# Attention, mixer and feed-forward in one kernel: 51 shifted due times in a planned order of work

## Chip, cores and metric

The kernel runs on one core of one Trainium2 chip. The metric is the device time of one execution in microseconds (us); less is better. The time before is a median of three runs.

## The reference

Three parts follow one another, all in float32. B = 8 batches, 8 heads, S = 576 positions, width 512.

```python
# attention: phi(x) = [exp(p), exp(-p)], p = x @ w_phi - max|x @ w_phi|
kv = einsum('bhsf,bhsd->bhfd', phi(k), v);  z = sum_s phi(k)
out = einsum('bhsf,bhfd->bhsd', phi(q), kv) / (einsum('bhsf,bhf->bhs', phi(q), z) + 1e-6)
# mixer: causal convolution of 5 taps as a gate
x = (sigmoid(conv(x, conv_w)) * (x @ w_val)) @ w_out
# Fourier mixing, layer norm, feed-forward of width 2048
u = x + real(fft(fft(x, axis=1), axis=2))
out = u + relu(layernorm(u) @ w_ch1) @ w_ch2
```

## The kernel before, in words

Products that need full precision are made of three reduced ones: a tile is split in a high half (a copy on ScalarE, `o_hi`) and a low half (a subtraction on VectorE or GpSimd, `o_lo`), and `mm3` issues high x high, high x low and low x high.

*The attention loop* (`run_attention`) is an order written out by hand: 49 stages, in each of which the projection, the exponentials, the products `kv` and `num`, the division and the transposes of different groups of the sequence overlap. Beside it the weights are converted.

*The joint list* is all that comes after: the last of the attention (`note_tail`: transposes `yt`, products `kv`, three times `num`, four times the transposes `xt` and their copy to `xT`), the mixer and the Fourier mixing for eight batches (`note_mix`), and the feed-forward part for five blocks of columns (`note_mlp`; its products are made with seven instead of eight quarter products, tiles `x`, `y`, `z`, `cx`, `cy`). The note functions don't issue anything. Each call of `op` appends a step to a list: which engines may do it (m TensorE, v VectorE, a ScalarE, p GpSimd, d a load or store), how long it is thought to take, the function that issues it, and the keys that it reads and writes. The list has some 4,600 steps. Steps are numbered in the order in which they are noted.

*The planner* (`place_ops`) turns the list into one order per engine. It works out from the keys which step needs which. A pass from the back then gives each step a due time, the latest at which it may start if all that follows it is to fit before the end; the pass is run twice, the second time with the ends of the five stages that the first one found. Then the list is dealt out from the front: each time, for every engine, of the steps that can start earliest the one with the earliest due time is a candidate, and the candidate with the earliest start of all is placed. A step that may run on VectorE or GpSimd goes to whichever takes it first. The order found is issued as it stands; each engine works its own instructions off in that order and waits where an input isn't there. So a due time sets which of several ready steps goes first, and nothing else.

The planner begins with `free`, the time at which each engine becomes free, and `key_at`, the time at which keys from before the list are ready. Both are zero here, although at that point the attention loop's last instructions still run.

In the mixer each batch's activations are split into the tile `xh` (four chunks, one buffer). For each of four column groups `val` = `xh` x `wv` is computed in two banks, multiplied by the gate `acc` (five taps on ScalarE and VectorE, then a sigmoid) into `gv`, folded into `gs` and split into `ge`. The products of `ge` with `wo`, then those with the Fourier tables, go to a ring of four banks `ps`. The layer norm of the first block (`ln_first`, in two halves) runs between the later batches; it reads back `u`, which was stored in `u_scr`.

`u<-x`, `f<-fs`, `ge<-gs`, `xh<-xf` and `r<-r` in the rows are such sums and splits. `ws<-s_scr` is a load of weights whose sums GpSimd makes.

Nearly all steps of the list have line 64 in the profile, as one helper issues them; they are told apart by their tiles.

Of the kernel before, what the change touches and what calls it, by code (L numbers as in the profile page):

```python
# [9 lines left out]
F32 = mybir.dt.float32  # L10
# [5 lines left out]
ACTF = mybir.ActivationFunctionType  # L16
# [51 lines left out]
def attention_moe_mixer_kernel(  # L68
# [19 lines left out]
    pe, act, vec, gps = (Issue(x) for x in (nc.tensor, nc.scalar, nc.vector, nc.gpsimd))  # L88
    mm = pe.matmul

    def pool(stack, name, bufs, space=None, side=None):
        kw = {} if space is None else {"space": space}
        if side is not None:
            kw["side"] = side
        if space is not DRAM:
            kw["reuse_waits"] = "tile"
        return stack.enter_context(tc.tile_pool(name=name, bufs=bufs, **kw))
# [96 lines left out]
    NG, CH = 3, 3  # L194
# [5 lines left out]
    early = ExitStack()  # L200
# [22 lines left out]
    sm_p = pool(att, "sm", 2)  # L223
# [14 lines left out]
    kvps = {}  # L238
    kvT = {}
    xs = {}  # L240
    xT = {}
# [39 lines left out]

    KV_PARTS = [[[(0, 0), (1, 1), (2, 2)]], [[(3, 0), (4, 1)], [(5, 1), (6, 2)]], [[(7, 0), (8, 1), (9, 2)]]]

    def emit_KV(i, part):
        u, g = divmod(i, NG)
        tv = vraw[u % 2]
        e = kE[i]
        for slot, j in KV_PARTS[g][part]:
            b = slot // 5
            if slot % 5 == 0:  # L290
                kvps[u, b] = ps_kv.tile([128, 4, 66], F32, tag="kv", name="kv")
            t = kvps[u, b]
            for h in range(2):
                for a in range(2):
                    w = 2 * h + a
                    for p in HALVES:
                        mm(t[p, w, :], e[:, a, h, j, p], tv[:, h, slot, :],
                           start=slot % 5 == 0 and w == 0, stop=slot % 5 == 4 and w == 3, skip_group_check=True)
            if slot % 5 == 4:
                if b == 0:  # L300
                    kvT[u] = sm_p.tile([128, 4, 2, 65], F32, tag="kvT", name="kvT")
                act.activation(out=kvT[u][:, :, b, :], in_=kvps.pop((u, b))[:, :, 0:65], func=ACTF.Copy)
        if part == len(KV_PARTS[g]) - 1:
            kE.pop(i)

    def emit_yT(i):
        y = yq.pop((i, 1))
        t = ps_tr.tile([128, 2, 512], F32, tag="tr", name="yt")
        for h in range(2):
            for j in range(CH):  # L310
                nc.tensor.transpose(t[:, h, j * F:(j + 1) * F], y[:, h, j, :], ident)  # L311
        yq[i, 2] = t

    def emit_qE(i, a):
        if a == 0:
            qE[i] = qe_p.tile([128, 2, 2, CH, F], F32, tag="qe", name="qe")
        t = yq[i, 2] if a == 0 else yq.pop((i, 2))
        act.activation(out=qE[i][:, a], in_=chunks(t), func=ACTF.Exp, scale=(1.0, -1.0)[a])

    def emit_num(i):  # L320
        u, g = divmod(i, NG)
        e = qE.pop(i)
        kt = kvT[u]
        nm[i] = t = ps_nm.tile([128, 2 * CH, 66], F32, tag="nm", name="nm")
        for j in range(CH):
            c = CH * g + j
            for h in range(2):
                for a in range(2):
                    for b, p in enumerate(HALVES):
                        if c != 4:  # L330
                            b = 0 if c < 4 else 1
                        mm(t[p, 2 * j + h, 0:65], e[:, a, h, j, p], kt[:, 2 * h + a, b, :],
                           start=(a == 0), stop=(a == 1))

    def emit_X(i):
        t = nm.pop(i)
        xs[i] = x = xs_p.tile([128, CH, 2, D], F32, tag="xs", name="xs")
        r = sm_p.tile([128, 2 * CH, 1], F32, tag="r", name="r")
        nc.vector.tensor_scalar(out=r, in0=t[:, :, D:D + 1], scalar1=1e-6, scalar2=None, op0=ALU.add)
        nc.vector.reciprocal(out=r, in_=r)  # L340
        nc.vector.tensor_tensor(
            out=x.rearrange("p c h d -> p (c h) d"), in0=t[:, :, 0:D], in1=r.to_broadcast([128, 2 * CH, D]), op=ALU.mult,
        )
# [8 lines left out]
    def emit_xT(i, e):  # L352
        t = xs.pop((i, 1))
        xT[i] = xT_p.tile([128, CH * F], F32, tag="xT", name="xT")
        (hi_dve if e == "v" else hi_act)(xT[i], t[:, 0, 0:CH * F])
# [307 lines left out]
    def stage(k):  # L663
        n = k if isinstance(k, str) else k[0]
        if n == "ge":
            n += str(k[1])
        if k == ("ps", 4) or k[:2] == ("x2", 1):
            return 3, 3
        return STAGES.get(n, (0, 4))
# [8 lines left out]
    def op(e, cols, fn, reads, writes, dur=None, more=0.0, two=False, table=None, kb=0):  # L678


        two = two and not any(k in BANKS or k[0] in BANKS for k in reads)
        if dur is None:
            dur = {k: COST[k][0] + COST[k][1] * cols / 1000 for k in e}
        else:
            dur = {e: dur}
        at = [stage(k) for k in reads + writes]
        ops.append((dur, fn, reads, writes, more, two, max([a for a, b in at], default=0), min([b for a, b in at], default=4), table, here[0], kb))
# [471 lines left out]
                c2 = c2_units(t, pair)  # L1159
        drain(c2)  # L1160

    key_at = {}
    free = dict.fromkeys("mvapdxw", 0.0)

    def place_ops():
        n = len(ops)
# [21 lines left out]
        part = [o[6] for o in ops]  # L1188
# [4 lines left out]
        due = [0.0] * n  # L1193
# [3 lines left out]
        for i in reversed(range(n)):  # L1197
            now -= ops[i][0].get("m", 0)
            if "m" in ops[i][0] or ops[i][9]:
                place[i] = now  # L1200
        for _ in range(2):
            till = dict.fromkeys("mvapdw", total)
            rest = [len(s) for s in succ]
            heap = []

            def open_up(i):
                late = min([due[s] - lat for s in succ[i]] + [ends[last[i]], total]) - ops[i][4]
                if ops[i][10]:
                    late = min(late, till["w"] - K["bw"] * ops[i][10])
                late = min(late, place[i] + min(ops[i][0].values()))  # L1210
                heapq.heappush(heap, (-late, -i))

            for i in reversed(range(n)):
                if not rest[i]:
                    open_up(i)
            while heap:
                late, i = (-k for k in heapq.heappop(heap))
                e = max(ops[i][0], key=lambda e: min(late, till[e]) - ops[i][0][e])
                due[i] = till[e] = min(late, till[e]) - ops[i][0][e]
                if ops[i][10]:  # L1220
                    till["w"] = min(till["w"], late + K["bw"] * ops[i][10]) - K["bw"] * ops[i][10]
                for p in pred[i]:
                    rest[p] -= 1
                    if not rest[p]:
                        open_up(p)
            ends = [min(due[i] for i in range(n) if part[i] > k) if k < 4 else 1e9 for k in range(5)]
        left = [len(p) for p in pred]
        ready = {e: set() for e in "mvapd"}
        at = [max([key_at.get(k, 0.0) + lat for k in ops[i][2] + ops[i][3]], default=0.0) for i in range(n)]
# [25 lines left out]
        for _ in range(n):  # L1255
            best = None
            for e, q in ready.items():
# [14 lines left out]
                i, t0 = min(((i, t) for i, t in cand if t <= t0 + K["win"]), key=lambda c: (due[c[0]], c[0]))  # L1272
# [41 lines left out]
    def note_tail():  # L1314
        nk = ["kvT"]

        def kv(i):
            op("m", 0, lambda e: emit_KV(i, 0), ["early"], ["kv"], 24 * 0.058)

        def yt(i):  # L1320
            op("m", 0, lambda e: emit_yT(i), ["early"], ["tr"], 2 * CH * 0.11)
            for a in range(2):
                op("a", 256 * CH, lambda e, a=a: emit_qE(i, a), ["tr", "att"], [("qe", i, a)], table=ACTF.Exp)

        def num(i):
            op("m", 0, lambda e: emit_num(i), nk * (i % NG > 0) + [("qe", i, 0), ("qe", i, 1), "att"], ["nm"], 8 * CH * 0.058)

        def x(i):
            op("v", 0, lambda e: emit_X(i), ["nm", "att"], [("xs", i % 3)], 0.19 + 0.2 + 0.07 + 0.13 * CH)

        def xt(i):
            op("m", 0, lambda e: emit_XT(i, ps_tr, "tr"), [("xs", i % 3), "att"], ["tr"], CH * 0.11)
            op("a", 128 * CH, lambda e: emit_xT(i, "a"), ["tr"], [("xT", i % 2)])
            t = Late(lambda: xT[i])
            o_dma([(o, t[:, k]) for b, o, k in x_parts(i)], [("xT", i % 2)], [("x_scr", b) for b, o, k in x_parts(i)], 192)

        yt(TOT - 1)
        kv(TOT - 1)
        num(TOT - 3)
        x(TOT - 3)  # L1340
        xt(TOT - 4)
        for i in range(TOT - 3, TOT):
            yield
            xt(i)
            if i + 1 < TOT:
                num(i + 1)
                x(i + 1)

    def run_attention():
# [8 lines left out]
        with tc.manual_schedule():  # L1358
            for st in range(TOT + 1):
# [6 lines left out]
                if two:  # L1366
                    emit_KV(st - 2, 0)
# [5 lines left out]
                if at(2):  # L1373
                    emit_KV(st - 2, int(two))
# [167 lines left out]
```

## Time and the profile before

| | before |
|---|---|
| median of three runs | 1323.23 us (1321.36 to 1324.6) |
| the profiled execution's own time | 1319.18 us |
| its span, first to last instruction | 1317.1 us |
| TensorE busy | 1285.5 us, 98% |
| VectorE busy | 1134.1 us, 86% |
| ScalarE busy | 919.0 us, 70% |
| GpSimd busy | 791.9 us, 60% |
| mean granted TensorE clock | 0.996 |

Engines in rows: PE is TensorE's matmuls, PEld its weight loads, DVE VectorE, ACT ScalarE, POOL GpSimd, SPq the queue that issues loads and stores. Times in the rows are from the span's start. The busy share of an engine that nobody waits for says nothing about the time; idle time of TensorE does.

### The profile page before, as it was taken

The numbers are of one execution on the slowest core, as the hardware profiler recorded it, in microseconds if no ns is written. First come the engines' busy times: TensorE is split into PE (matmuls) and PEld (weight loads), VectorE is DVE, ScalarE is ACT, GpSimd is POOL, SyncE is SP. The second block draws the span as 40 slices with busy tenths as digits, with TensorE's granted clock in tenths as the row PEclk, the third lists the DMA queues.
The fourth block names the chain that finished last, engine by engine and source line by source line (L and its number), as shares of the span: only waits on it lengthen the run. The fifth ranks groups of instructions, "written<-read, shape, count | busy, mean of one in ns | idle before, by whom it ended". The sixth has DMA issues, their size and how long they took to land.

```text
span 1317.1 us, 30740 instructions
## 1 busy us (share of the span) xinstructions
PE 1285.5 (98%) x11952; PEld 1183.3 (90%) x11952; DVE 1134.1 (86%) x1771; ACT 919.0 (70%) x1718; POOL 791.9 (60%) x661
## 2 busy tenths in 40 slices
PE   8999999998999998999999999999999999999998
PEld 7999899988999998998888888888888888889997
DVE  6888888878889889779989989998989888888785
ACT  6888999774556546466867687767677676777662
POOL 4868889333557666464665755597458856583321
PEclk9999999998999999999999999999999999999999
DMA  8689999522342442528433653356333743345322
GB/s 309 207 287 308 319 300 296 189 83 89 137 165 88 147 155 89 177 89 276 138 102 102 222 159 104 103 160 218 104 103 117 241 123 100 105 149 182 105 84 89
DMA packets 147005, 214.62 MB, mean 163 GB/s; under 512 B 18854, under 2 KB 105382, under 8 KB 146860
## 3 DMA queue, kind: packets, MB, share of 16 engines
q1 hardware_dynamic: 142400, 203.06, 47.5%
q10 hardware_dynamic: 4460, 9.62, 2.0%
q8 instruction: 93, 1.52, 0.5%
q14 instruction: 52, 0.43, 0.1%
HBM read 165.63 MB, written 46.99 MB: 161 GB/s over the span
## 4 chain that ended last, share of the span: by engine, by line
PE 86%; DVE 6%; ACT 4%; DMA 2%; issue 1%; POOL 0%; SPq 0%; DVEq 0%; POOLq 0%; ACTq 0%
PE x L64 15%; PE cx L64 15%; PE ps L64 12%; PE cy L64 11%; PE y L64 8%; PE val L64 5%; PE kv L64 5%; PE pj L64 5%; PE nm L64 4%; PE z L64 4%; DVE acc L64 2%; PE yt L311 2%; PE xt L349 1%; ACT qe L64 1%; DMA r<-s_scr 1%
## 5 line engine op out<-in xcount | busy, mean ns | idle before, releaser
L64 POOL TENSOR_TENSOR r<-r 128x256 fp32r<-128x256 f32 (+1 forms) x301 | 293.4, 992 | 245.6 <-ACT r L64 229.2
L64 ACT ACTIVATE r<-r 128x256 fp32r<-128x256 f32 (+1 forms) x420 | 195.3, 487 | 53.4 <-DMA r<-s_scr 49.7
L64 PE MATMUL x<-un,r 128*128 128x462 f32 (+1 forms) x960 | 221.2, 371 | 2.2 <-ACT c L64 1.4
L64 PE MATMUL cx<-h,r 128*128 128x462 f32 (+1 forms) x960 | 213.9, 371 | 1.1 <-DVE acc L64 1.1
L64 PEld LDWEIGHTS x<-un,r 128*128 128x128 f32 x960 | 180.4, 188 | 23.5 <-ACT c L64 1.8
L64 PEld LDWEIGHTS cx<-h,r 128*128 128x128 f32 x960 | 180.2, 188 | 22.1 <-DVE acc L64 1.8
L64 PE MATMUL cy<-h,r 128*128 128x462 f32 (+1 forms) x720 | 159.9, 370 | 0.0
L64 PEld LDWEIGHTS cy<-h,r 128*128 128x128 f32 x720 | 135.3, 188 | 15.1
L64 PE MATMUL val<-xh,wv 128*128 128x290 f32 x768 | 118.0, 303 | 10.6 <-DVE gs L64 4.7
L64 PEld LDWEIGHTS val<-xh,wv 128*128 128x128 f32 x768 | 108.5, 193 | 13.7 <-DVE gs L64 5.6
L64 PE MATMUL y<-un,r 128*128 128x462 f32 (+1 forms) x480 | 113.9, 372 | 0.4 <-DVE h L64 0.4
L64 PE MATMUL ps<-ge,wo 128*128 128x290 f32 x768 | 107.3, 297 | 2.0 <-DVE x L64 1.1
L64 PEld LDWEIGHTS ps<-ge,wo 128*128 128x128 f32 x768 | 104.5, 189 | 2.8 <-DVE x L64 1.3
L270 DVE TENSOR_REDUCE m<-pj 128x6 f32<-128x768 f32 x96 | 91.5, 953 | 15.4 <-PE pj L64 14.8
L64 PEld LDWEIGHTS y<-un,r 128*128 128x128 f32 x480 | 90.0, 188 | 11.4 <-DVE h L64 1.1
L64 DVE SCALAR_TENSOR_TENSOR acc<-xf,cw,acc 128x576 f32<-128x576 f32 x112 | 91.4, 816 | 10.0 <-ACT acc L64 9.1
L64 DVE TENSOR_TENSOR acc<-cx,acc 128x924 f32<-128x924 f32 (+1 forms) x80 | 88.9, 1112 | 11.6 <-PE cx L64 10.2
L271 DVE TENSOR_TENSOR y<-pj,m 128x768 f32<-128x768 f32 x96 | 91.9, 958 | 6.9 <-DVE m L270 0.5
L64 PE MATMUL kv<-vraw,ke 128*64 128x66 f32 x2560 | 88.1, 224 | 1.7 <-ACT kvT L64 1.7
L64 ACT ACTIVATE qe<-yt 128x768 f32<-128x768 f32 x96 | 72.6, 812 | 23.4 <-PE yt L311 23.4
L64 ACT ACTIVATE h<-z 128x462 fp32r<-128x462 f32 (+1 forms) x120 | 66.4, 553 | 29.8 <-DVE z L64 26.1
L64 PE MATMUL pj<-wp,kqraw 64*128 64x128 f32 x1152 | 80.8, 287 | 6.0 <-DMA kqraw<-in_k_dram 4.0
(174 smaller groups left out, 2752.5 us busy)
## 6 DMA issues: line engine op xcount, KB each, us to landing
r<-s_scr SPq DMA_DIRECT2D x280, 128.0 KB, 2.4
r<-s_scr SPq DMA_DIRECT2D x140, 256.0 KB, 2.6
raw<-in_w_ch_dram SPq DMA_DIRECT2D x32, 512.0 KB, 6.0
vraw<-in_v_dram SPq DMA_DIRECT2D x32, 330.0 KB, 6.1
u_scr<-u ACTq DMA_DIRECT2D x8, 1152.0 KB, 6.3
kqraw<-in_k_dram SPq DMA_DIRECT2D x46, 192.0 KB, 4.1
kqraw<-in_q_dram SPq DMA_DIRECT2D x46, 192.0 KB, 3.7
s_scr<-mt SPq DMA_DIRECT2D x32, 256.0 KB, 5.2
```

What stands on the lines that cost most here:

```text
L64: return lambda *a, **k: f(*(resolve(x) for x in a), **{n: resolve(x) for n, x in k.items()})
L270: nc.vector.tensor_reduce(out=m, in_=pv, axis=AX.X, op=ALU.max, apply_absolute_value=True)
L271: nc.vector.tensor_tensor(out=y, in0=pv, in1=m.unsqueeze(3).to_broadcast([128, 2, CH, F]), op=ALU.subtract)
L311: nc.tensor.transpose(t[:, h, j * F:(j + 1) * F], y[:, h, j, :], ident)
L349: nc.tensor.transpose(t[:, 0, j * F:(j + 1) * F], x[:, j].rearrange("p h d -> p (h d)"), ident)
```

## The change

Five edits, all in how the list is noted and planned. The due times of 51 numbered steps are shifted after the passes, by half of the table's number in us (negative: due earlier). The planner is told that ScalarE becomes free at 1.4, VectorE at 0.7, and the bank `tr` at 1.4. The backward pass runs three times. The copy of the last `kvT`, which was issued together with the products `kv`, becomes a step of its own on ScalarE (so that steps behind the fourth have numbers greater by one than before). The copy to `xT` may go to VectorE or ScalarE.

```diff
+    def copy_KV(u, b):
+        if b == 0:
+            kvT[u] = sm_p.tile([128, 4, 2, 65], F32, tag="kvT", name="kvT")
+        act.activation(out=kvT[u][:, :, b, :], in_=kvps.pop((u, b))[:, :, 0:65], func=ACTF.Copy)
+
-    def emit_KV(i, part):
+    def emit_KV(i, part, copy=True):
...
-            if slot % 5 == 4:
-                if b == 0:
-                    kvT[u] = sm_p.tile([128, 4, 2, 65], F32, tag="kvT", name="kvT")
-                act.activation(out=kvT[u][:, :, b, :], in_=kvps.pop((u, b))[:, :, 0:65], func=ACTF.Copy)
+            if slot % 5 == 4 and copy:
+                copy_KV(u, b)
...
-    key_at = {}
-    free = dict.fromkeys("mvapdxw", 0.0)
+    MOVES = {
+        7: 100, 55: -40, 72: 68, 87: 70, 88: 151, 110: -35, 122: -347, 129: -11, 131: 9, 132: 59, 159: 47, 200: -98,
+        218: 5, 309: 9, 322: 22, 376: 70, 395: -87, 402: 8, 428: -10, 433: 20, 448: -156, 463: -52, 482: -80, 485: 68,
+        511: -24, 578: 4, 601: 31, 620: -30, 662: 186, 699: 15, 701: -17, 792: -167, 798: -147, 810: -39, 823: -27,
+        910: -339, 916: 8, 1001: 9, 1059: -50, 1094: 8, 1117: 3, 1164: 95, 1182: 13, 1239: 174, 1243: 291, 1287: 260,
+        1399: 112, 1405: 41, 1431: -25, 1498: -255, 1523: 17,
+    }
+    key_at = {"tr": 1.4}
+    free = dict(dict.fromkeys("mvapdxw", 0.0), a=1.4, v=0.7)
...
-        for _ in range(2):
+        for _ in range(3):
...
+        for i, v in MOVES.items():
+            due[i] += 0.5 * v
...
-            op("m", 0, lambda e: emit_KV(i, 0), ["early"], ["kv"], 24 * 0.058)
+            op("m", 0, lambda e: emit_KV(i, 0, False), ["early"], ["kv"], 24 * 0.058)
+            op("a", 260, lambda e: copy_KV(i // NG, 1), ["kv"], ["kvT"])
...
-            op("a", 128 * CH, lambda e: emit_xT(i, "a"), ["tr"], [("xT", i % 2)])
+            op("va", 128 * CH, lambda e: emit_xT(i, e), ["tr"], [("xT", i % 2)])
```

Some of the shifted steps, by their numbers: 7 is the first group of transposes `xt`; 87 and 88 are the low half of the second chunk and the high half of the third of `xh` for the second batch; 122 is a tap of the gate for the same batch; 792 (a sum on GpSimd) and 798 (a subtraction on VectorE) belong to the first block's layer norm; 910 is a low half of `f` on GpSimd; 1498 is the copy of a product to the tile `c11` on ScalarE, at the beginning of the feed-forward part.

## Rows read from the trace of the kernel before

**Rows 1.** The page's first and fourth part: busy time, and the chain's shares.
```profile
span 1317.1 us, 30740 instructions
...
PE 1285.5 (98%) x11952; PEld 1183.3 (90%) x11952; DVE 1134.1 (86%) x1771; ACT 919.0 (70%) x1718; POOL 791.9 (60%) x661
...
PE 86%; DVE 6%; ACT 4%; DMA 2%; issue 1%; POOL 0%; SPq 0%; DVEq 0%; POOLq 0%; ACTq 0%
```

**Rows 2.** Busy time by stretch: length, engines (instructions), granted clock, DMA share, GB/s.
```profile
0.00:285.00 285.00, 277.25 (x6230) 256.19 (x6230) 239.70 (x375) 242.20 (x323) 200.12 (x113) 1.00 0.78 259
285.00:310.00 25.00, 22.91 (x314) 21.42 (x312) 18.31 (x41) 13.85 (x21) 3.50 (x5) 1.00 0.39 135
310.00:321.00 11.00, 7.03 (x33) 6.58 (x31) 8.74 (x15) 4.20 (x8) 8.37 (x8) 0.69 0.24 83
321.00:350.00 29.00, 27.19 (x201) 26.75 (x201) 23.41 (x46) 15.45 (x30) 16.97 (x20) 1.00 0.28 97
350.00:480.00 130.00, 128.29 (x963) 126.52 (x962) 117.34 (x226) 73.94 (x152) 78.98 (x70) 1.00 0.42 145
480.00:510.00 30.00, 24.05 (x173) 22.83 (x172) 26.46 (x47) 16.45 (x30) 18.89 (x18) 1.00 0.30 101
510.00:605.00 95.00, 95.00 (x700) 93.12 (x699) 79.81 (x133) 53.27 (x127) 56.55 (x47) 1.00 0.36 127
605.00:610.00 5.00, 2.84 (x13) 1.91 (x12) 4.27 (x9) 4.11 (x10) 1.91 (x2) 1.00 1.01 349
610.00:1300.00 690.00, 688.53 (x3286) 617.06 (x3287) 608.91 (x881) 495.25 (x1022) 405.80 (x380) 1.00 0.45 139
```

**Rows 3.** Waits of TensorE's matmuls from 285 us on: total, times, longest.
```profile
PE val L64 <- DVE gs L64: 4.7, 3, 3.2
PE val L64 <- DVE xh L64: 4.2, 2, 2.6
PE yt L311 <- ACT qe L64: 1.6, 1, 1.6
...
PE x L64 <- ACT c L64: 1.4, 1, 1.4
PE xt L349 <- ACT xT L64: 1.3, 1, 1.3
```

**Rows 4.** Timeline of 276 to 325 us, some instructions: start, duration, idle before.
```profile
287.80 0.87 PE L311 MATMUL yt<-ident,y 128*128 128x128 f32 x6 [1.60 <-ACT qe L64]
...
290.27 0.39 ACT L64 ACTIVATE kvT<-kv 128x260 f32<-128x260 f32 x1 [2.52 <-PE kv L64]
...
291.22 1.50 ACT L64 ACTIVATE qe<-yt 128x768 f32<-128x768 f32 x2
291.32 3.40 DVE L64 SCALAR_TENSOR_TENSOR acc<-x,cw,acc 128x576 f32<-128x576 f32 x4 [4.30 <-ACT acc L64]
...
308.84 2.41 ACT L64 ACTIVATE xh<-xf 128x576 fp32r<-128x576 f32 x4
...
310.18 4.14 POOL L64 TENSOR_TENSOR xh<-xf,xh 128x576 fp32r<-128x576 f32 x3
...
313.62 1.31 DVE L64 TENSOR_TENSOR xh<-xf,xh 128x576 fp32r<-128x576 f32 x1
...
314.99 5.92 PE L64 MATMUL val<-xh,wv 128*128 128x290 f32 x23 [2.63 <-DVE xh L64]
```

**Rows 5.** Timeline of 478 to 515 us, some instructions.
```profile
478.25 0.75 DVE L64 TENSOR_TENSOR xh<-xf,xh 128x576 fp32r<-128x576 f32 x1
...
480.57 1.00 POOL L64 TENSOR_TENSOR x<-x 128x462 f32<-128x462 f32 x1 [2.41 <-DMA x<-u_scr]
...
488.93 1.02 ACT L64 ACTIVATE x<-ps 128x290 f32<-128x290 f32 x3 [3.67 <-POOL u L64]
```

**Rows 6.** Timeline of 596 to 614 us, some instructions.
```profile
609.22 0.57 ACT L64 ACTIVATE c<-x 128x462 f32<-128x462 f32 x1
...
609.84 1.53 PE L64 MATMUL x<-un,r 128*128 128x462 f32 x6 [1.43 <-ACT c L64]
```

## Prediction

> **What bounds the kernel now.** I read the page first. TensorE is busy for 1285.5 of 1317.1 us and the chain that ended last runs through it for 86% of the span [rows 1]. So the change can only win where TensorE stands still or runs slowly, and I asked for the busy time stretch by stretch [rows 2]. The reader is to look at the PE column against the length of each stretch, and at the number of matmuls.
>
> - 0 to 285 is the attention loop, written out by hand. It holds 285 - 277.25 = 7.75 us of idle TensorE, but the change doesn't touch it.
> - 285 to 310 is where the joint list takes over: 25 - 22.91 = 2.09 idle.
> - 310 to 321 is the worst place: 11 - 7.03 = 3.97 idle, and a granted clock of 0.69, so part of it at 1.2 GHz and not 2.4.
> - 321 to 350: 1.81. 350 to 480: 1.71. 480 to 510: 5.95. 510 to 605: nothing. 605 to 610: 2.16.
> - 610 to 1300, the feed-forward part: 1.47 in 690 us. From 1300 on there is the last drain, in which no order can help.
>
> Between 285 and 1300 that is 2.09 + 3.97 + 1.81 + 1.71 + 5.95 + 2.16 + 1.47 = 19.2 us. To this comes the slow clock. The 23 matmuls that follow the hole at 310 took 5.92 us [rows 4]; in 510 to 605 one matmul costs 95 / 700 = 0.136 us [rows 2], so 23 should take 3.1, and 2.8 are lost. The ceiling is 19.2 + 2.8 = 22 us, 1.7%. Nothing else is to be had, as no matmul goes away.
>
> Then the waits of TensorE [rows 3]: `val` products wait for `gs` and for the low halves of `xh`, which VectorE makes; the transposes of `yt` wait for `qe`; an `x` product waits for the copy `c`. All are waits for work on another engine that a different order could bring earlier, none is a wait for a load. That is the kind of idle time that due times can touch.
>
> **The change part by part.** No instruction is added or removed, but for an engine that can differ for four copies. What changes is the order in which the list hands steps to each engine, and that order is binding: whatever stands ahead in an engine's program waits in front of everything behind it.
>
> *How the attention leaves its engines.* Before, the list thought all engines free at its start. TensorE's first step was the transposes `yt`, which stood 1.60 us for the `qe` copies that still held the bank [rows 4]. With `tr` given as free at 1.4 and ScalarE at 1.4, `yt` costs a wait and the ready `kv` products go first. I take the whole 1.6; the ends are 0 (another ready step is chosen that also waits) and 2.09.
>
> *The copy of `kvT` as a step of its own.* Before, it was issued together with the `kv` products, so ScalarE met it early and stood 2.52 us for them, with `acc` and `qe` (at 291.22) behind it; VectorE in turn stood 4.30 us for `acc` [rows 4]. As a step it comes when the products are planned to be done. Up to 2.5 us on ScalarE, and as much on VectorE's start; on TensorE nothing by itself, as it has `val` products there. The gain shows only if it reaches the hole at 310. What the two products of `num` behind it wait for is the same copy: if it now comes later than 290.27 they go later, at no cost while `val` products cover them.
>
> *`xT` on either engine, four copies.* VectorE or ScalarE takes them; TensorE's wait for one is at most 1.3 [rows 3]. I count nothing: VectorE has little room there, and a copy moved to it would push what TensorE needs.
>
> *The hole at 310 to 321.* The tile `xh` has one buffer. When the first batch's last `val` product is done, ScalarE writes four high halves (2.41 us for all), then four low halves follow, three on GpSimd (4.14) and one on VectorE (1.31), and TensorE starts 2.63 after it last had work [rows 4]. What fills this time now is only the rest of the attention's transposes. Of the first 200 steps twelve are moved: a transpose `xt` later (number 7, by 50 us), the third chunk's high half and the second's low half later (88 and 87), a tap of `acc` earlier (122, by 174). They keep work that needs no `xh` for the hole, or put VectorE's chain first. With the earlier start of VectorE I take half, 2.0 of 3.97; the ends are 0 and 3.97. If the hole is halved the clock should hold: in 480 to 510 TensorE stood 3.2 in one piece [rows 3] and the granted clock stayed 1.00 [rows 2]. So I add the 2.8, with 0 as its other end. The page TensorE: Matmul & The Clock Gate of the Trainium skill, section "Part 1: The HAM clock gate (the 'warmup' mystery)", says the same of the two levels: idleness takes the clock to 1.2 GHz and sustained activity brings it back. By it too, a shorter hole pays more than its own length; the sum doesn't change.
>
> *The other moves.* Of the 51 moved steps 46 lie in the mixing stages and five behind them. 26 are matmul groups, 17 lie on VectorE or GpSimd, 7 on ScalarE and one is a store; 11 are moved by 5.5 us or less. For 321 to 350 I take half of 1.81, 0.9; for 350 to 480 0.5 of 1.71, as it is small pieces. In 480 to 510 ScalarE stood 3.67 for GpSimd's `u`, which itself came behind a load that GpSimd had waited 2.41 for [rows 5]. Steps 792, 798 and 910 (two of the layer norm on GpSimd and VectorE, one low half of `f` on GpSimd) are pulled forward by 84, 74 and 170 us here. Half: 3.0, ends 0 and 5.95. At 605 to 610 step 1498 is the copy `c` on ScalarE that ran at 609.22, behind four writes of `h`, and for which TensorE stood 1.43 [rows 6]; it is pulled forward by 128 us, so it goes first as soon as its bank is full. The two pieces there cannot both go; I take 0.8 of 2.16.
>
> *The third pass over the due times* moves all 4,600 of them a little, those of the feed-forward part too. It has 1.47 us to win there in 690, and what it can lose is hidden as long as VectorE keeps its room (608.91 busy of 690). I take nothing, with a loss of 1.5 and a gain of 1.47 as its ends.
>
> *The sum.* 1.6 + 2.0 + 2.8 + 0.9 + 0.5 + 3.0 + 0.8 = 11.6. Against it goes one new stall of the size of today's `yt` wait, 1.6, because a new order rarely takes only the old waits: 10.0 us. The profiled execution took 1319.18 us (2.08 outside its span), so it would be 1309.2; it lies 4 us below the median of the three runs, so from the median 1323.2 I get **1313 us**.
>
> **The rivals.**
>
> *VectorE becomes the bound.* In 480 to 510 it is busy for 26.46 of 30 and in 310 to 321 for 8.74 of 11 [rows 2]. If TensorE's waits are only its shadow, no order gives more than VectorE's own idle time there, 3.5 and 2.3. With half of these, the entry's 1.6 and 0.8 at 605, and the clock still lost: 1.8 + 1.1 + 1.6 + 0.8 = 5.3, 1318 us. For it: TensorE's longest waits are for VectorE. Against: some of VectorE's work there (taps of the next batch) isn't urgent. The port makes it worse: a low half on VectorE took 1.31 while GpSimd ran (it ended just after GpSimd's three) [rows 4] and 0.75 when GpSimd was idle [rows 5]. The Trainium skill's page SBUF — State Buffer, section "Who interferes with whom", has this as a rule: a VectorE instruction with two SBUF inputs and a GpSimd one that reads SBUF block each other for a whole instruction. By that rule moves that pair more of them would cost 0.56 each on VectorE; the trace agrees with the rule in these two rows.
>
> *The holes only move.* Due times decide between steps that are ready together; the list is late throughout, and other waits of the same sort take the place of the old. 1323 us. For it: five kinds of wait are named [rows 3], for the work of two engines. Against: the entry and step 1498 answer to waits that are plain in the trace.
>
> *Slower: the layer norm's steps come before their load.* Step 792 on GpSimd reads what a load from `u_scr` brings, and it is pulled forward. If it stands in GpSimd's program before the load has landed, GpSimd waits, its `u` and `f` behind it, then ScalarE's evictions, as at 480 to 510 now [rows 5]. One more stretch like that one costs its 5.95 again: 1323.2 + 6 = 1329 us with nothing recovered. It decides when idle TensorE in 350 to 610, now 1.71 + 5.95 + 2.16 = 9.8, exceeds about 14. Against: GpSimd waited for such a load 2.41 us only.
>
> *Nearly all is recovered.* 20 of 22 us: 1303. Against: the single buffer of `xh` stays, so its hole can be filled, not closed.
>
> **How the numbers follow.** About 4 us, 0.3%, is what a measurement can tell from no change. Half recovered (1309 to 1317) 0.45; nearly all 0.10; VectorE the bound 0.15, of which 0.12 beyond 4 us; holes only move 0.17; slower 0.13. Faster: 0.45 + 0.10 + 0.12 = 0.67; same 0.03 + 0.17 = 0.20; slower 0.13. The range is 1305 to 1324: it leaves out most of the slower case and most of the best one, some 0.18.
>
> **What would show it.** Right: at the list's start `kv` ahead of `yt` and no wait of 1.6; `kvT` on ScalarE without 2.5 us of waiting; a granted clock of 1.00 at 310 to 321; idle TensorE in 480 to 510 of about 3; the wait for `c` near 610 gone; 610 to 1300 as before. Wrong: the clock still falls, or the feed-forward part holds over 3 us of idle TensorE, or a new wait for a load on GpSimd with ScalarE behind it.

## The result, and the profile after

The changed kernel takes 1301.21 us in the median (1299.25 to 1302.63, four runs) against 1322.3 (1320.0 to 1324.6): a ratio of 0.984, interval 0.982 to 0.986. That is 21 us less, where 10 were forecast, and outside the range of 1305 to 1324. The rival "nearly all is recovered" is what happened.

The profiled execution took 1302.1 us. First the page, busy time and the chain's shares, which answer to [rows 1]:

```profile
span 1300.3 us, 30757 instructions
...
PE 1281.4 (99%) x11952; PEld 1181.0 (91%) x11952; DVE 1130.3 (87%) x1773; ACT 917.2 (71%) x1719; POOL 786.9 (61%) x660
...
PE 86%; ACT 5%; DMA 4%; DVE 4%; issue 0%; POOL 0%; SPq 0%; POOLq 0%; DVEq 0%; ACTq 0%
```

Then busy time by stretch, as in [rows 2]:

```profile
285.00:310.00 25.00, 23.19 (x316) 21.87 (x316) 20.02 (x42) 17.40 (x26) 6.49 (x8) 1.00 0.41 143
310.00:321.00 11.00, 10.60 (x67) 10.57 (x68) 10.39 (x20) 3.56 (x6) 4.48 (x4) 0.84 0.32 108
321.00:350.00 29.00, 29.00 (x221) 28.93 (x221) 27.52 (x55) 17.32 (x36) 16.96 (x20) 1.00 0.32 105
350.00:480.00 130.00, 129.36 (x973) 128.13 (x973) 122.55 (x229) 76.02 (x155) 91.61 (x82) 1.00 0.43 150
480.00:510.00 30.00, 30.00 (x227) 29.65 (x226) 28.59 (x55) 21.67 (x44) 21.94 (x20) 1.00 0.30 110
510.00:605.00 95.00, 94.76 (x652) 91.15 (x651) 77.78 (x135) 55.39 (x133) 42.83 (x38) 1.00 0.49 164
605.00:610.00 5.00, 4.92 (x24) 4.07 (x23) 3.11 (x6) 3.69 (x9) 2.07 (x3) 1.00 1.07 370
```

Two wider stretches, in each pair the kernel before first and the changed one second:

```profile
285.00:350.00 65.00, 57.13 (x543) 54.74 (x541) 50.46 (x100) 33.49 (x58) 28.84 (x32) 0.95 0.31 109
285.00:350.00 65.00, 62.78 (x602) 61.37 (x603) 57.93 (x115) 38.28 (x67) 27.93 (x31) 0.97 0.36 120
...
615.00:1290.00 675.00, 673.53 (x3215) 603.56 (x3213) 596.00 (x862) 485.71 (x1002) 402.05 (x377) 1.00 0.45 139
615.00:1290.00 675.00, 672.80 (x3210) 602.63 (x3209) 592.59 (x851) 476.88 (x984) 397.20 (x372) 1.00 0.43 133
```

The reader is to compare the first number behind each length with the length. Idle TensorE between 285 and 610 was 17.7 us and is 3.2. The worst stretch, 480 to 510, has no idle time at all, and TensorE issued 227 matmuls there instead of 173, while VectorE went from 26.46 to 28.59 busy: it had room, and the earlier order hadn't used it. The feed-forward part won nothing: from 615 to 1290 TensorE stands 2.20 us where it stood 1.47.

The waits of TensorE's matmuls from 284 us on, the longest (total, times, longest one), which answer to [rows 3]:

```profile
PE val L64 <- DVE xh L64: 2.0, 1, 2.0
PE cx L64 <- DVE acc L64: 1.0, 2, 0.6
PE y L64 <- DVE h L64: 1.0, 1, 1.0
PE x L64 <- ACT r L64: 0.9, 1, 0.9
PE val L64 <- POOL xh L64: 0.6, 1, 0.6
```

The waits for `gs`, `qe`, `xT` and `c` are gone. Two waits are new or longer, both in the feed-forward part: the one for `r` (at 614.68 us) and the one for `h` (1.03 at 654.63; the longest such wait before was 0.4). The entry and the hole behind it in the timeline, as in [rows 4]:

```profile
286.02 1.62 PE L64 MATMUL kv<-vraw,ke 128*64 128x66 f32 x48
...
288.19 0.39 ACT L64 ACTIVATE kvT<-kv 128x260 f32<-128x260 f32 x1
...
288.97 0.88 PE L314 MATMUL yt<-ident,y 128*128 128x128 f32 x6
...
292.47 1.51 ACT L64 ACTIVATE qe<-yt 128x768 f32<-128x768 f32 x2
...
307.01 1.82 ACT L64 ACTIVATE xh<-xf 128x576 fp32r<-128x576 f32 x3
...
308.33 3.30 POOL L64 TENSOR_TENSOR xh<-xf,xh 128x576 fp32r<-128x576 f32 x2 [1.67 <-ACT xh L64]
308.36 1.98 DVE L64 TENSOR_TENSOR xh<-xf,xh 128x576 fp32r<-128x576 f32 x1
...
310.40 4.90 PE L64 MATMUL val<-xh,wv 128*128 128x290 f32 x23 [1.99 <-DVE xh L64]
...
315.14 1.79 PE L64 MATMUL ps<-ge,wo 128*128 128x290 f32 x12
```

`kv` goes before `yt`, and neither waits; `kvT` is copied without ScalarE standing for it. The transposes `xt` stand between `val` products up to 308 us. The hole in front of `xh` is 1.99 us, and the second batch's 23 `val` products behind it begin at 310.40 instead of 314.99.

### The profile page after: what moved, and what is told of

Read it like the earlier page. It is cut to its first block, busy times and chain, and to the rows that moved or that the text cites. A ratio compares the mean times of both kernels' runs of the same rounds, so it can differ in the third digit from the quotient of the medians.

```text
span 1300.3 us, 30757 instructions
## 1 busy us (share of the span) xinstructions
PE 1281.4 (99%) x11952; PEld 1181.0 (91%) x11952; DVE 1130.3 (87%) x1773; ACT 917.2 (71%) x1719; POOL 786.9 (61%) x660
## 4 chain that ended last, share of the span: by engine, by line
PE 86%; ACT 5%; DMA 4%; DVE 4%; issue 0%; POOL 0%; SPq 0%; POOLq 0%; DVEq 0%; ACTq 0%
PE x L64 15%; PE cx L64 15%; PE cy L64 11%; PE ps L64 11%; PE y L64 8%; PE val L64 7%; PE kv L64 5%; PE pj L64 4%; PE nm L64 4%; PE z L64 4%; PE yt L314 2%; PE xt L352 1%; DMA r<-s_scr 1%; ACT qe L64 1%; DMA x<-u_scr 1%; DVE acc L64 1%
## 5 line engine op out<-in xcount | busy, mean ns | idle before, releaser
L64 POOL TENSOR_TENSOR r<-r 128x256 fp32r<-128x256 f32 (+1 forms) x305 | 296.7, 990 | 246.7 <-ACT r L64 226.9
L64 PE MATMUL val<-xh,wv 128*128 128x290 f32 x768 | 115.2, 301 | 2.9 <-DVE xh L64 2.0
```

Source lines behind the costliest of these rows:

```text
L64: return lambda *a, **k: f(*(resolve(x) for x in a), **{n: resolve(x) for n, x in k.items()})
```

## The experiments

Each kernel was timed in five rounds beside the kernel before on the same chip. The changed kernel's ratio, 0.984, stands for comparison.

**1. The other four edits, without the shifts.**

```diff
-        for i, v in MOVES.items():
-            due[i] += 0.5 * v
```

> The changed kernel without the 51 shifts; its other four edits stay. Theory A (the shifts close the holes of TensorE, the other edits only set the stage): 1317 to 1323 us, with idle TensorE of 4 us or more again in the stretch about 480 to 510 us and a slow clock about 315. Rival B (it is the handover and the third pass that close them, the shifts add little): 1301 to 1306 us and no hole of over 2 us between 285 and 610.

1313.38 us against 1321.89, ratio 0.994 (0.992 to 0.995): between the two theories, 8 us of the gain without any shift. The stretches of its profile, from 285 us on:

```profile
285.00:350.00 65.00, 60.42 (x585) 58.46 (x582) 56.18 (x113) 35.87 (x59) 27.85 (x30) 0.97 0.37 125
350.00:450.00 100.00, 98.89 (x743) 97.62 (x742) 88.32 (x166) 59.09 (x124) 69.31 (x62) 1.00 0.42 147
450.00:510.00 60.00, 58.41 (x433) 56.80 (x433) 57.89 (x113) 37.62 (x77) 40.74 (x38) 1.00 0.38 129
510.00:580.00 70.00, 69.01 (x520) 68.25 (x520) 51.74 (x93) 37.99 (x88) 35.32 (x28) 1.00 0.35 124
580.00:615.00 35.00, 32.28 (x179) 28.93 (x178) 27.43 (x51) 23.49 (x56) 18.07 (x17) 1.00 0.68 232
```

Idle TensorE of 4.6, 1.1, 1.6, 1.0 and 2.7 us. The hole about 500 that was expected back isn't there: this plan hasn't got it in the first place.

**2. The shifts alone, in the kernel before.**

```diff
+    MOVES = {
...
+    }
...
+        for i, v in MOVES.items():
+            due[i - 1] += 0.5 * v
```

> The kernel before with the 51 shifts alone (numbers moved down by one, as the copy of kvT is no step of its own here). Theory A1 (a shift is worth what it is worth, whatever the other edits): about 1304 to 1308 us. Theory A2 (the shifts fit one single plan, and every other plan takes them as noise): 1318 to 1326 us, holes in other places.

1320.52 us, ratio 1.000 (0.998 to 1.001). Nothing is won. Three of the same stretches:

```profile
285.00:350.00 65.00, 58.54 (x594) 56.28 (x589) 52.87 (x106) 35.18 (x61) 27.06 (x30) 0.97 0.33 112
...
450.00:510.00 60.00, 57.02 (x414) 55.64 (x414) 55.97 (x106) 32.62 (x70) 35.23 (x33) 0.97 0.42 142
...
580.00:615.00 35.00, 29.95 (x187) 27.91 (x186) 26.04 (x47) 18.74 (x47) 17.32 (x15) 0.90 0.45 148
```

The idle time is somewhere else: 5 us lie in 580 to 615, and an `x` product waits 5.0 us once for the copy `c`, a wait of the kind that step 1498's shift takes away in the changed kernel.

**3. Changed, but with all engines given as free at zero.**

```diff
-    key_at = {"tr": 1.4}
-    free = dict(dict.fromkeys("mvapdxw", 0.0), a=1.4, v=0.7)
+    key_at = {}
+    free = dict.fromkeys("mvapdxw", 0.0)
```

> The changed kernel with all engines and the bank of the transposes given as free at zero again, all else as changed. If the handover is worth only its own wait: 1.6 us more than the changed kernel, about 1303 us. If the shifts fit one plan only (A2): 1310 to 1320 us, with idle TensorE not at the entry alone but also after 450 us, where the handover has long passed.

1315.56 us, ratio 0.995 (0.994 to 0.997). Its profile has the entry's 1.6 us back, and 6.1 idle in 450 to 510. Two lines that concern the first two microseconds of the list decide about 14 us.

**4. The same amounts on the wrong steps.**

```diff
-        for i, v in MOVES.items():
+        for i, v in zip(sorted(MOVES), list(MOVES.values())[1:] + [100]):
```

> The changed kernel with the same 51 steps and the same 51 amounts, each amount given to the next step of the table. A: shifts of this size without the search are harmful or do nothing: 1318 to 1332 us. B: as the shifts matter little, 1301 to 1306 us.

1325.49 us, ratio 1.003 (1.002 to 1.004), slower than before. Shifts of this size are no help as such, as far as one such mixture can show.

**5, 6, 7. Some of the shifts left out.**

```diff
+            if i in (792, 798, 910):
+                continue
```

> The changed kernel without the shifts of steps 792, 798 and 910 (layer norm and one low half of f). Theory A1 (each shift heals the place where its step stands): idle TensorE of 3 to 6 us again between 470 and 510 us and none elsewhere; 1304 to 1307 us. A2 (any missing shift sends the whole list behind it another way): holes behind 510 too, about 1306 to 1315 us.

1306.23 us, ratio 0.988 (0.985 to 0.990); by the times alone it can't be told from the changed kernel (0.982 to 0.986). The traces differ, here the changed kernel's stretch first:

```profile
450.00:510.00 60.00, 59.36 (x445) 58.67 (x444) 57.32 (x109) 36.33 (x72) 42.78 (x39) 1.00 0.35 117
450.00:510.00 60.00, 57.05 (x418) 55.07 (x417) 55.46 (x107) 33.76 (x65) 38.40 (x37) 1.00 0.39 126
```

Idle TensorE is 2.95 us against 0.64, and in every other stretch up to 615 us within 0.7 us of the changed kernel's: these three act where they stand.

```diff
+            if i == 1498:
+                continue
```

> The changed kernel without the shift of step 1498 alone. A1: TensorE waits 1.4 us or so for the copy c once, about 590 to 605 us, and nothing else changes: 1302 to 1303 us, a difference that the times can hardly show and the trace can. A2: more than 3 us.

1305.32 us, ratio 0.987 (0.985 to 0.989); the interval overlaps the changed kernel's, so the times don't tell a difference of 1.4 us from one of over 3. The trace has the wait that the shift takes away, once, and no other of over 1.1 us:

```profile
PE x L64 <- ACT c L64: 1.3, 1, 1.3
```

```diff
+            if i <= 200:
+                continue
```

> The changed kernel without the twelve shifts of the first 200 steps. A1: the hole about 310 us is back at 3 to 4 us with a slow clock behind it, and the stretches from 350 us on are as in the changed kernel: 1304 to 1307 us. A2: 1308 to 1318 us, with idle TensorE after 450 us, where none of the twelve steps is at work any more.

1312.45 us, ratio 0.992 (0.990 to 0.994). Most of what the shifts add is lost, although 39 of the 51 are still there:

```profile
285.00:350.00 65.00, 59.57 (x583) 57.85 (x583) 56.95 (x114) 38.02 (x63) 27.57 (x31) 1.00 0.37 125
...
450.00:510.00 60.00, 55.84 (x398) 53.76 (x397) 58.89 (x109) 34.63 (x70) 40.85 (x37) 0.97 0.39 130
```

5.4 us idle to 350, as expected by either; but also 4.2 in 450 to 510, more than with no shift at all (1.6 in the first experiment). The hole of 3 to 4 us about 310 is back, but the slow clock that was expected behind it isn't: 1.00 from 285 to 350.

**8. The rest of the hole filled.** Twelve more matmuls into a bank that is about to be overwritten; what they compute is used nowhere.

```diff
-                def prod(e, p=p, sl=sl, part=part):
+                def prod(e, p=p, sl=sl, part=part, n=n):
...
+                    if (b, m, n, part) == (1, 0, 0, (0, 1)):
+                        for r in range(12):
+                            mm(p[:, 0:NE], wv[0][:, 0, ws], wv[0][:, 0, 0:NE], start=True, stop=True)
```

> The changed kernel with 12 more matmuls of 290 columns on TensorE in the hole that is left at about 308.4 us, ahead of the second batch's first val product and into the bank that it overwrites; their result is used nowhere. If the slow clock behind the hole comes of the idle time: granted clock 1.00 throughout 305 to 320, the 23 matmuls behind it in 3.1 instead of 4.9 us, so 1.5 to 1.8 us less than the changed kernel, about 1299.5 us. If the clock falls for another reason: no gain, or 1.6 us lost where the added matmuls stand ahead of ready work, about 1301 to 1303.

1301.76 us, ratio 0.984 (0.981 to 0.986). The times show no gain, but a gain of the 1.5 us that was forecast lies within that interval. The stretches about the hole, and three rows of its timeline:

```profile
308.00:311.00 3.00, 3.00 (x24) 3.00 (x24) 2.80 (x4) 3.00 (x7) 1.67 (x2) 1.00 0.35 121
311.00:314.00 3.00, 2.30 (x16) 1.82 (x15) 3.00 (x7) 1.80 (x3) 2.24 (x3) 1.00 0.18 66
...
308.54 1.82 ACT L64 ACTIVATE xh<-xf 128x576 fp32r<-128x576 f32 x3
...
311.96 0.94 PE L64 MATMUL val<-xh,wv 128*128 128x290 f32 x5 [0.39 <-DVE xh L64]
...
315.75 1.79 PE L64 MATMUL ps<-ge,wo 128*128 128x290 f32 x12
```

The granted clock stayed at 1.00 (2.4 GHz), as forecast for the first theory. This execution came to the hole late: the split of `xh` began 1.53 us later than in the changed kernel's profile (308.54 against 307.01). The `ge` products behind the hole began only 0.61 later (315.75 against 315.14), so 0.9 us came back there, of 1.5 to 1.8 forecast. That both profiled executions have a span of 1300.3 us says nothing against this; the last section has more.

**9, 10, 11. Which of the other edits gives the 8 us.** The handover alone; the handover, the `kvT` step and the free `xT` (two passes); the third pass, the `kvT` step and the free `xT` (no handover). None has the shifts. Against the kernel before, the first is

```diff
-    key_at = {}
-    free = dict.fromkeys("mvapdxw", 0.0)
+    key_at = {"tr": 1.4}
+    free = dict(dict.fromkeys("mvapdxw", 0.0), a=1.4, v=0.7)
```

and the other two are the first experiment's kernel with

```diff
-        for _ in range(3):
+        for _ in range(2):
```

and with the third experiment's edit.

> The kernel before with the handover alone (ScalarE free at 1.4, VectorE at 0.7, the bank of the transposes at 1.4). If the gain of 8 us that is left without the shifts is the handover's: about 1313 to 1316 us. If it takes the edits together: 1318 to 1325, the wait of 1.6 us at the entry gone, and holes of other sizes behind it.

> The changed kernel without the shifts and with two passes instead of three: the handover, the copy of kvT as a step and the free engine of xT are left. If the third pass gives nothing: about 1313 us as with it. If it gives a part: 1316 to 1322 us, with idle TensorE about 500 us.

> The changed kernel without the shifts and without the handover: the third pass, the copy of kvT and the free engine of xT are left. If each edit is a reordering of its own that heals the place it stands at: about 1318 us. If orders are as good as drawn by lot between these edits: 1318 to 1328 us, either side of the kernel before.

Ratios 0.996 (0.995 to 0.998), 1.000 (0.998 to 1.001) and 1.001 (0.9995 to 1.002). The handover alone wins 5 us; with two more edits, for which the prediction counted nothing, nothing is left; with the third pass on top it is 8. The eleventh kernel waits at one place longer than the kernel before at any:

```profile
PE val L64 <- DVE gs L64: 7.9, 3, 6.8
```

So these edits aren't terms of a sum. Each gives another order, with holes of other sizes at other places. The expectation of the ninth named either all 8 us or none, and missed.

**12. The first twelve shifts only.**

```diff
+            if i > 200:
+                continue
```

> The changed kernel with only the twelve shifts of the first 200 steps. If a shift acts from its own place on and the later ones mend what follows: busy TensorE to 350 us as in the changed kernel (idle of about 2 us in 285 to 350, against 7.9 before), then holes again about 490 to 510 and 580 to 615 us; 1308 to 1314 us. If the early shifts only work with the later ones: idle of 4 us or more before 350, 1314 to 1322 us.

1312.72 us, ratio 0.993 (0.991 to 0.995), as its first theory had it:

```profile
285.00:350.00 65.00, 63.42 (x629) 61.46 (x624) 57.79 (x118) 39.03 (x71) 30.79 (x33) 1.00 0.36 125
...
450.00:510.00 60.00, 56.74 (x406) 55.02 (x405) 57.10 (x108) 34.05 (x66) 40.46 (x38) 0.97 0.37 126
...
580.00:615.00 35.00, 32.28 (x165) 28.79 (x164) 26.86 (x49) 22.79 (x50) 16.33 (x15) 0.95 0.75 254
```

1.6 us idle to 350, then 3.3 and 2.7 where the later shifts would have been at work. Together with experiments 5 to 7 this fits the reading that early shifts change everything behind them, and that a later one mends only what the earlier have left. It isn't shown for each shift: only 16 of the 51 were left out in groups or singly.

## Why the prediction was wrong

**What bounds the kernel** was right: the ceiling of 22 us, made of idle TensorE and slow clock from 285 on, held, and nearly all that was won was won before 610; the feed-forward part lost 0.7 us.

**The entry** was right in what happens: the wait of 1.6 us is gone, `kv` comes first, `kvT` without a wait. **The hole at 310** was 3.97 in two pieces, and is 1.99 in one: the half that was forecast. The second batch's 23 `val` products behind it start 4.6 us earlier. The granted clock still fell in the profiled execution (0.84), and 23 matmuls took 4.90 us: 1.0 of the 2.8 came back, not all. "If the hole is halved the clock should hold" is refuted for this execution. From 285 to 350 us the kernel before issued 543 matmuls and the changed one 602; 59 more, at 0.13 us (130 us for 973 in 350 to 480), make 7.7 us. So these terms and that for 321 to 350, 7.3 together, were about right.

**What failed is the term for 350 to 510, "Half: 3.0, ends 0 and 5.95", with the 0.5 ahead of it; a smaller miss is the 0.8 of 2.16 at 605 to 610.** From 350 to 510 the kernel before issues 963 + 173 matmuls [rows 2] and the changed one 973 + 227: 64 more, at 0.13 us 8.4 us against 3.5 forecast, so 4.9 too little. (Idle time, 7.66 us before and 0.64 after, shows 7.0 of it.) At 605 to 610 idle time went from 2.16 to 0.08: both pieces went, which the prediction held to be impossible, and 1.3 more came back than it took. The 1.6 for a new stall was about right in size: TensorE now stands 0.24 us in 510 to 605, 0.88 at 614.68 and 0.73 more than before from 615 to 1290, 1.85 in all. With the 0.4 to 350 us, 4.9 + 1.3 + 0.4 - 0.25 makes 6.35 of the 7.1 us that the profiled pair's 17.1 exceeds the forecast of 10.0.

I had taken the half as the middle between ends that were far apart; no row spoke for it. What the rows did say was that these waits were for VectorE's and ScalarE's work, and that VectorE had 3.5 of 30 us free there. They set no floor at half: the changed order closed that stretch's hole whole.

The other 4 us lie outside any term: the profiled execution of before took 1319.18 and its median over all runs is near 1322, the changed kernel's 1302.1 and 1301.2. What a slower execution of the kernel before does in these us wasn't profiled and stays open. The granted clock goes with it in part: of the 69 executions of that kernel timed beside the experiments, the 26 with a mean clock of 0.997 or more took 1320.5 us on average, and the 25 with 0.995 or less 1323.8. The four of the changed kernel have 0.998 and 0.999.

**The premise under the sum**, that each edit is worth something at its own place, holds only for late shifts taken singly or by threes (experiments 6 and 5: 1.3 and 2.3 us in the trace, where the term for step 1498 said 0.8). It fails for everything early: shifts alone 0.0%, the other edits alone 0.6%, together 1.6%; and 14 us hang on the handover, which was priced at 1.6. **The rivals:** VectorE as the bound is refuted for the worst stretch (28.59 busy of 30, TensorE 30.00). "The holes only move" is refuted for this set of edits and is just what experiments 2, 10 and 11 show for parts of it. "The layer norm's steps come before their load" didn't occur: idle TensorE in 350 to 610 is 1.0 us, where that rival asked for 14. The single buffer of `xh` did keep one hole, as said against the rival that won.

## What to carry to other kernels

Where all the idle time of the engine that bounds the kernel is waiting for other engines' work, and those engines have room, a reordering can get back far more than half of it (here 14.5 of 17.7 us). So a set of constants that fits the whole plan is to be judged by the ceiling, unless a row speaks for less. Such constants belong to one plan: here taking back an edit to the first steps undid about two thirds of the whole gain, and in the kernel before they gave nothing. So they are to be tested again after every other change, and parts of such a change can't be tested one by one and added up. In this list the early steps decided most; look at them first.

## What the runs showed that was not expected

*Who gets at `xh` first.* At the hole, GpSimd and VectorE each begin a low half of `xh` within 0.03 us of each other, and executions with the same instructions of these two at this place differ in which of them goes on. In the changed kernel's profile VectorE's took 1.98 us. In experiment 6, with the same order here, it took 0.75 and GpSimd's pair longer:

```profile
310.22 3.98 POOL L64 TENSOR_TENSOR xh<-xf,xh 128x576 fp32r<-128x576 f32 x2 [1.41 <-ACT xh L64]
310.24 0.75 DVE L64 TENSOR_TENSOR xh<-xf,xh 128x576 fp32r<-128x576 f32 x1
311.04 0.67 PE L64 MATMUL val<-xh,wv 128*128 128x290 f32 x3 [0.76 <-DVE xh L64]
```

There the one hole becomes two of 0.76 and 0.60 us, and the granted clock stays 1.00; experiment 12 has nearly the same (0.76 and 0.61, clock 1.00). In the changed kernel and in experiment 5 VectorE loses, the hole is 1.99 us in both, and the clock falls to 1.2 GHz behind it. Experiment 8 had VectorE lose (2.02), the twelve matmuls in the hole, and the clock at 1.00. The Trainium skill's page SBUF — State Buffer, section "SBUF: two separate sides", says that of such a pair the one that starts first has the shared port for its whole instruction, and the other blocks. The traces agree on the whole instruction: GpSimd's first low half took 1.40 us where VectorE's took 1.98 (0.75 and most of that 1.40), and 2.04 where VectorE's took 0.75. On who comes first the recorded starts don't tell: GpSimd's is the earlier by 0.02 or 0.03 us in all five traces, also in the two in which VectorE went on.

*What became of a late start.* By 285 us the changed kernel had issued 6230 matmuls, and experiments 8 and 6, with the same attention loop, only 6185 and 6171. In experiment 6 the split of `xh` began 1.89 us later than in the changed kernel (308.90 against 307.01), and the `ge` products behind the hole at the same time (315.10 against 315.14):

```profile
308.90 1.82 ACT L64 ACTIVATE xh<-xf 128x576 fp32r<-128x576 f32 x3
...
315.10 1.79 PE L64 MATMUL ps<-ge,wo 128*128 128x290 f32 x12
```

In experiment 8 TensorE went on with `xh` as much later as the split had begun (311.96 against 310.40), and 0.9 us came back only behind that, where the changed kernel's matmuls ran at 1.2 GHz. So in both the lateness was made good, in part or whole, behind the hole, with the clock at 1.00 and, in experiment 6, VectorE first. That experiment 8 ends level with the changed kernel rests on waits elsewhere too: it hasn't got the 0.88 at 614.68 and the 1.03 at 654.63, and stands 1.65 once at 872.36. Why these differ stays open.

*The clock* fell after a hole of 1.99 us here, and held in the kernel before through one of 3.2 at 504 to 507. The nearest pair are experiments 1 and 7, in this order, with almost the same hole before the same product:

```profile
312.32 1.81 PE L64 MATMUL val<-xh,wv 128*128 128x290 f32 x11 [3.23 <-DVE xh L64]
...
310.95 1.76 PE L64 MATMUL val<-xh,wv 128*128 128x290 f32 x11 [3.25 <-DVE xh L64]
```

In the first the granted clock fell (0.97 in 285 to 350), in the second it held (1.00). The length of one hole alone doesn't tell.
